# Last MoE1 block with its output product two tiles behind, layer 2's first weights loaded at once, y loads moved up

## The chip, the cores and the metric

One core of one Trainium2 chip runs the whole program in one launch. The metric is the device time of one execution in microseconds, as the median of several runs. The profile is one execution, taken by the hardware profiler. TensorE (PE) multiplies matrices; VectorE (DVE), ScalarE (ACT) and GpSimd (POOL) do the elementwise work; SyncE's queue (SP) issues nearly all DMAs. Each engine runs its own queue in order.

## The reference, cut to what matters

```python
attn_out = _attn_ref(q, k, v)                      # pooled + local attention, (4, 8, 576, 64)
x = attn_out.transpose(0, 2, 1, 3).reshape(2304, 512)
# MoE1: 512 -> 1536 -> 512
g = x @ w_gate
silu = g * (1.0 / (1.0 + np.exp(-g)))
y = silu * (x @ w_val) @ w_out
# MoE2 (layer 2): 512 -> 2048 -> 512
h = y @ w_in
g = np.maximum(h, 0.0) + alpha * np.minimum(h, 0.0)
out = g @ w_out2
```

Activations are float32 and the weights are float64, read on the chip as pairs of 32-bit words.

## The kernel before

**Products.** A float32 product is made of three TensorE products of operands split into a high and a low part: hi x hi, hi x lo, lo x hi (L488 to L490 in MoE1, L875 to L877 in layer 2). The high part is a cast on ACT, the low part a subtraction on POOL. Each float64 weight tile is first put together as float32: two ACT passes over the raw words (L656, L660), a merge on DVE (L664), then cast and subtraction (L687, L691). A loaded and split weight tile lives in a named SBUF place, `g0` to `g11`, `v0` to `v11`, `o0` to `o11`; a raw load (`w_load`) and its split result take places of that list.

**MoE1.** The tokens are 8 blocks of 288. For each block and each of 12 feature tiles j of 128: `m_g` (12 products, then `u`: tanh on ACT L531 and a DVE operation L532), `m_v` (12 products, then `u` on DVE L539, `ph` on ACT L542, `pl` on POOL L543), and `m_y`, the output product of the tile before (12 products into the PSUM tiles `Y`). So the order on TensorE is g(j), v(j), y(j-1). In the last block, g and v have four PSUM banks instead of two. The block's result is copied (L565) and written to `y1` in DRAM (L566).

**Layer 2, first product.** It runs as steps (token pair-block i of 576, weight pair q of 256 features), 32 of them, in the order of `VISITS`: i=0 with q 0 to 3, i=1 with q 0 to 7, i=0 with q 4 to 7, then i=2 and i=3. A step uses the seven-product scheme P1 to P7 of 2x2 blocks: six TensorE products each, with copies on ACT between them (L911 behind P1, L929 behind P6, L920 behind P7, L940 behind P5). `close` adds P4 and P3 of the step before, `prelu` applies the activation on DVE (L892, L893) and stores to `hbuf`. Its operands are sums and differences of weights (`conv_w`, L695 to L702) and of y (`prep_y`, L810, cast L796, low part L803 or L806). They are prepared in the background from the last MoE1 block on. For q above 4 the sums and differences of the weights run on POOL, else on DVE. The second product is `m2_out`, with weights from `conv_o`.

**The planner.** From the last MoE1 block on, the order on every queue is the order in which the program emits instructions. Background work is a list of tasks with engine, cost, inputs, earliest time `at` and due time. `tick` advances a planned clock (0.80 us for six products of 288 columns; it starts at 0 with the block) and `run_bg` goes through the tasks in order of due time: a task is emitted when its inputs are planned to end within LA and its engine is planned to be free within LB.

```python
COST = dict(A=lambda n: 0.2 + 0.00075 * n, D=lambda n: 0.14 + 0.0011 * n, P=lambda n: 0.05 + 0.0025 * n, S=lambda n: 5.0)
...
                if t["at"] > now or any(d["end"] is None or d["end"] > now + LA for d in t["deps"]):
                    continue
                if t["e"] != "S" and free.get(t["e"], 0.0) > now + LB:
```

`S` is a load: its cost is the planned time until the data have landed. A0 is the planned start of layer 2. `prod` forces whatever it needs that has not been emitted. Places: `PAIR` names, for each weight pair, the places of its raw loads and of its results, `X5S` those of its P7 operand, `YS` those of the first set of y operands.

Of the kernel before, what the change touches and what calls it, by code (L numbers as in the profile page):

```python
# [10 lines left out]
I32 = mybir.dt.int32  # L11
# [12 lines left out]
def attn_moe_moe2_kernel(  # L24
# [72 lines left out]
    wdma = {}  # L97
    W = {}

    def w_load(kind, j, slot):  # L100
        t = raw[slot] = wp.tile([128, 512, 2], I32, tag=slot, name="raw")
        src = wsrc[kind]
        if kind in ("o", "o2"):
            r = nc.sync.dma_start(out=t.rearrange("p f t -> p (f t)"), in_=src[j * 128:(j + 1) * 128, :])
        else:
            r = nc.sync.dma_start(
                out=t.rearrange("p f t -> p (f t)").rearrange("p (k f) -> p k f", k=KD),
                in_=src[:, j * 256:(j + 1) * 256].rearrange("(k p) f -> p k f", p=128))
        wdma[slot] = r.ins
# [424 lines left out]
    def m_v(blk, j):  # L534
        xh, xl = xt(blk)
        G = GB[2 * (j % 2) + 1] if blk == NB1 - 1 else GV[1]
        proj(G, HB, W[f"v{j}"][:, 0], W[f"v{j}"][:, 1], xh, xl)
        u = hid.pop((blk, j))
        nc.vector.scalar_tensor_tensor(out=u, in0=u, scalar=0.5, in1=G[:, :HB], op0=ALU.mult, op1=ALU.mult)  # L539
        ph = hp_.tile([128, HB], F32R, tag="ph", name="ph")  # L540
        pl = hp_.tile([128, HB], F32R, tag="pl", name="pl")
        nc.scalar.copy(out=ph, in_=u)  # L542
        nc.gpsimd.tensor_sub(pl, u, f32(ph))  # L543
        hid[blk, j] = (ph, pl)

    def m_y(blk, j):
# [7 lines left out]
        if j == F1 - 1:  # L554
# [16 lines left out]
    NQ = F2 // 2  # L571
    TB = 2 * HB
    NB2 = NT // TB
    PAIR = [("v0", "g1", "o0"), ("v1", "g2", "o1"), ("g3", "v3", "o2"), ("g4", "v4", "o3"),
            ("g8", "v8", "o7"), ("g9", "v9", "o8"), ("g10", "v10", "o9"), ("g11", "v11", "o10")]
    X5S = ["g0", "v2", "v7", "o11"]
    YS = ["g5", "v5", "o4", "o5", "g6", "v6", "g7", "o6"]
    VISITS = [(0, 0, 4), (1, 0, 8), (0, 4, 8), (2, 0, 8), (3, 0, 8)]
    YSET = (0, 1, 1, 0)
    GB = []  # L580
    SETS = []
    hbuf = dp.tile([F2 * 128, NT], F32, name="hbuf")

    A0 = 59.2
    LA, LB = 0.6, 0.8
    clock = [0.0]
    free = {}
    tasks = []
    due = [0.0]
    COST = dict(A=lambda n: 0.2 + 0.00075 * n, D=lambda n: 0.14 + 0.0011 * n, P=lambda n: 0.05 + 0.0025 * n, S=lambda n: 5.0)  # L590

    def bg(eng, n, fn, *deps, at=0.0):
        t = dict(e=eng, d=COST[eng](n), fn=fn, deps=deps, at=at, end=None, due=due[0])
        tasks.append(t)
        tasks.sort(key=lambda x: x["due"])
        return t

    def run_bg(flush=False):
        now = clock[0]
        busy = set()  # L600
        for t in list(tasks):
            if not flush:
                if t["e"] in busy:
                    continue
                if t["at"] > now or any(d["end"] is None or d["end"] > now + LA for d in t["deps"]):
                    continue
                if t["e"] != "S" and free.get(t["e"], 0.0) > now + LB:
                    busy.add(t["e"])
                    continue
            start = max([now, 0.0 if t["e"] == "S" else free.get(t["e"], 0.0)] + [d["end"] for d in t["deps"]])  # L610
            t["end"] = start + t["d"] + 0.15
            if t["e"] != "S":
                free[t["e"]] = start + t["d"]
            tasks.remove(t)
            t["fn"]()
# [15 lines left out]
    def tick(n, w):  # L631
        clock[0] += n * (0.0096 + 0.0004286 * w)
        run_bg()
# [10 lines left out]
    def unpack(kind, j, slot, which):  # L644
        z = {}

        def load():
            w_load(kind, j, slot)
            z["r"] = raw.pop(slot)

        def bits():
            n = 768 if which else 512
            z["t"] = side2.tile([128, n], F32, tag=f"st{which}", name="st", bufs=1)
            st = z["st"] = z["t"][:, 0:512]
            hw = z["r"][:, :, 1]
            nc.scalar.activation(out=st, in_=hw.bitcast(F32), func=AF.Prelu, scale=2.0 ** -112, alpha=-2.0 ** 32)  # L656

        def top():
            z["sk"] = side2.tile([128, 512], I32, tag="sk", name="sk", bufs=1)
            nc.scalar.activation(out=z["sk"], in_=top_byte(z["r"]), func=AF.Copy, scale=1.0 / 32, bias=-31.0 / 64)  # L660

        def merge():
            sti = z["st"].bitcast(I32)
            nc.vector.scalar_tensor_tensor(out=sti, in0=sti, scalar=3, in1=z["sk"],  # L664
                                           op0=ALU.logical_shift_left, op1=ALU.bitwise_or)

        return z, load, bits, top, merge

    def conv_w(q, at):
# [2 lines left out]
        s = PAIR[q]  # L672
        z0, load0, bits0, top0, merge0 = unpack("i2", 2 * q, s[0], 0)
        z1, load1_, bits1, top1, merge1 = unpack("i2", 2 * q + 1, s[1], 1)
        home = (s[2], s[1], s[0])
        x = {}
        val = {0: lambda: z0["st"], 1: lambda: z1["t"][:, 256:768], 2: lambda: z0["v"], 5: lambda: z1["t"][:, 0:256]}

# [44 lines left out]
        o1 = bg("P", 512, lo(1), h1)  # L723
        o2 = bg("P", 512, lo(2), h2)
        wt[q] = dict(P1=o0, P2=o0, P4=o1, P5=o1, P6=o2, P3=o2, P7=o5)
        held.update(st0=[h0, o0, df], st2=[h2, o2], st1=[h1, o1, h5, o5, df], sk=[m_])

    def conv_o(q, at):
        due[0] = A0 + 179.2 + 11.0 * q
        s = PAIR[q]  # L730
        ops = []
        for e, home in ((0, s[2]), (1, s[0])):
            z, load, bits, top, merge = unpack("o2", 2 * q + e, s[e], e)

            def hi(z=z, home=home):
                z["w"] = wp.tile([128, 2, 512], F32R, tag=home, name="w2")
# [38 lines left out]
    def prep_y(i, at, late, late0=None):  # L775
# [56 lines left out]
        o5 = bg("P", n, lo("P5", "11"), h5)  # L832
        yt[i] = dict(P1=o1, P2=o2, P3=o3, P7=o7, P6=o6, P4=o4, P5=o5)
        held["kn"] = [o7, o6, o4, o5]

    def again_p5(i, at, late):
        due[0] = late
# [70 lines left out]
    def step(s):  # L908
# [4 lines left out]
        tick(6, HB)  # L913
        if s:
            close(s - 1)

        def p7():
            prod(c, i, q, "P7", False)
            e = E7[s] = side2.tile([128, HB], F32, tag="e7", name="e7", bufs=2)
            nc.scalar.copy(out=e, in_=c)  # L920
            crit("A", 288, 0.8)
            tick(6, HB)

        if s == 0:
            p7()
            m_y(*fts[-1])
            open2()
        prod(t, i, q, "P6", True)
# [5 lines left out]
        tick(6, HB)  # L934
        prod(a, i, q, "P2", True)
        tick(6, HB)
        if s:
            p7()
        prod(b_, i, q, "P5", True)
        nc.scalar.copy(out=c, in_=b_)  # L940
        crit("A", 288, 0.8)
# [45 lines left out]
    if True:  # L987
# [141 lines left out]
        for i, (blk, j) in enumerate(fts):  # L1129
            if blk == NB1 - 1 and j == 0:  # L1130
# [5 lines left out]
                GB += [GV[0], GV[1], *[pa2.tile([128, 512], F32, name=f"h{e}") for e in range(2)]]  # L1136
                ctx.enter_context(tc.manual_schedule())
                live.append(1)
                for q in range(3):
                    conv_w(q, 0.8 * (10 + 9 * q))  # L1140
                prep_y(0, 0.8 * 26, 0.0, (29.6, 39.2))
                for q in range(3, 6):
                    conv_w(q, 0.8 * (37, 55, 61)[q - 3])
            if blk == 0:
                while pc[0] <= min(j + K["early"], F1 - 1):
                    prep1(pc[0])
# [17 lines left out]
            if last:  # L1164
# [1 line left out]
                crit("A", 288, 0.8)  # L1166
                crit("P", 288, 1.4)
                tick(6, HB)
            if i > 0:
                m_y(*fts[i - 1])  # L1170
            run(3 * i + 2)
            if last:
                tick(6, HB)
        gstack.close()
        pa3 = ctx.enter_context(tc.tile_pool(name="pa3", bufs=1, space=PSUM))
        SETS += [tuple(pa3.tile([128, 2, 512], F32, name=f"c{e}") for e in range(2)), (Y[0], Y[1])]
# [9 lines left out]
        for v, (i, q0, q1) in enumerate(VISITS):  # L1186
            now, end = clock[0], clock[0] + 5.58 * (q1 - q0)
            if v == 0:
                prep_y(1, now + 3.0, end + 1.6)
                for q in range(6, NQ):  # L1190
                    conv_w(q, now)
            elif v == 1:
                again_p5(0, end - 12.0, end)
                prep_y(2, end, end + 5.58 * 4)
            elif v == 3:
                prep_y(3, now, end)
# [49 lines left out]
```

## Time and profile before

| | us |
|---|---|
| median of 3 runs | 1003.16 |
| lowest and highest | 1002.13 and 1003.58 |
| the profiled execution | 1002.88 |
| its span, first to last instruction | 1001.1 |
| TensorE busy | 956.8 (96%) |
| VectorE, ScalarE, GpSimd busy | 494.6, 382.0, 458.5 |
| mean granted TensorE clock | 0.99 of full |

All times in the rows count from the start of the span. The last MoE1 block begins at 541.18. TensorE's products are pipelined: each row's length is longer than the distance of two starts, so the pace is read from the starts.

### The profile page before, as it was taken

To read this page: it belongs to the slowest core of one execution; us is meant where nothing else is said; L and a number is where in the kernel's file an instruction comes from. 1 tells how busy PE (TensorE), PEld (TensorE's weight loads), DVE (VectorE), ACT (ScalarE), POOL (GpSimd) and SP (SyncE) were. 2 spreads that over 40 slices of the span, in tenths; PEclk is the share of its full clock that TensorE was granted. 3 is DMA by queue.
4 is the path that set the end of the run, shared out by engine and by line. 5 is a ranking of instruction groups with operands and counts; after the bars stand their busy time and mean duration, and the time that the engine had idled before them with its cause. 6 is when DMAs were issued, how large, how long until landed. Compare 5 with 4: busy or idle time off the path is not lost.

```text
span 1001.1 us, 20369 instructions
## 1 busy us (share of the span) xinstructions
PE 956.8 (96%) x8144; PEld 883.8 (88%) x8144; DVE 494.6 (49%) x990; ACT 382.0 (38%) x876; POOL 458.5 (46%) x551
## 2 busy tenths in 40 slices
PE   5699899999999999999999988999999999999998
PEld 4589789999999999999999987999999887888886
DVE  5886874464535554444531564778566741010010
ACT  5698632222222222222222546544334574131231
POOL 6488853234322334222221586854511297444542
PEclk9989999999999999999999998999999999999999
DMA  7999731132111221111101644252425773353242
GB/s 192 266 335 332 176 89 34 27 80 58 37 42 33 69 47 41 45 23 20 43 9 41 200 126 137 96 190 95 143 107 204 246 241 123 89 184 99 91 131 100
DMA packets 151702, 116.22 MB, mean 116 GB/s; under 512 B 98873, under 2 KB 130617, under 8 KB 150841
## 3 DMA queue, kind: packets, MB, share of 16 engines
q1 hardware_dynamic: 151543, 114.92, 37.9%
q8 instruction: 63, 1.03, 0.4%
q14 instruction: 32, 0.26, 0.1%
q10 hardware_dynamic: 64, 0.01, 0.0%
HBM read 86.58 MB, written 34.60 MB: 121 GB/s over the span
## 4 chain that ended last, share of the span: by engine, by line
PE 76%; DVE 6%; DMA 6%; SPq 4%; POOL 3%; issue 3%; ACT 2%; DVEq 0%; POOLq 0%; ACTq 0%
PE y L488 7%; PE y L490 7%; PE y L489 7%; PE g L488 4%; PE v L489 4%; PE v L488 4%; PE g L489 4%; PE g L490 4%; PE v L490 4%; PE c L490 4%; PE c L489 4%; PE c L488 4%; PE c L875 3%; PE y L875 3%; PE c L876 3%
## 5 line engine op out<-in xcount | busy, mean ns | idle before, releaser
L961 POOL TENSOR_TENSOR hs<-hr,hs 128x512 fp32r<-128x512 f32 x72 | 96.6, 1358 | 84.8 <-ACT hs L960 84.8
L543 POOL TENSOR_TENSOR pl<-u,ph 128x288 fp32r<-128x288 f32 x96 | 81.5, 849 | 81.5 <-ACT ph L542 81.2
L489 PE MATMUL y<-pl,w 128*128 128x288 f32 x384 | 115.4, 302 | 2.5 <-POOL pl L543 2.5
L488 PE MATMUL g<-xh,w 128*128 128x288 f32 x360 | 109.9, 305 | 8.1 <-DVE u L532 3.8
L532 DVE SCALAR_TENSOR_TENSOR u<-u,g 128x288 f32<-128x288 f32 x90 | 40.7, 452 | 150.9 <-ACT u L531 150.7
L488 PE MATMUL y<-ph,w 128*128 128x288 f32 x384 | 113.1, 305 | 1.8 <-ACT ph L542 1.8
L490 PE MATMUL y<-ph,w 128*128 128x288 f32 x384 | 114.3, 300 | 0.0
L488 PE MATMUL v<-xh,w 128*128 128x288 f32 x360 | 108.9, 303 | 0.1
L489 PE MATMUL v<-xl,w 128*128 128x288 f32 x360 | 108.4, 301 | 0.0
L490 PE MATMUL g<-xh,w 128*128 128x288 f32 x360 | 107.3, 298 | 1.2 <-POOL qT L294 1.2
L489 PE MATMUL g<-xl,w 128*128 128x288 f32 x360 | 107.4, 298 | 0.0
L490 PE MATMUL v<-xh,w 128*128 128x288 f32 x360 | 106.8, 297 | 0.2 <-POOL w L143 0.2
L960 ACT CAST hs<-hr 128x512 fp32r<-128x512 f32 x72 | 41.7, 617 | 112.1 <-PE y L489 98.5
L531 ACT ACTIVATE u<-g 128x288 f32<-128x288 f32 x90 | 36.7, 408 | 122.4 <-PE g L490 118.9
L542 ACT CAST ph<-u 128x288 fp32r<-128x288 f32 x96 | 41.4, 432 | 104.8 <-DVE u L539 104.7
L981 DVE COPY os<-c 128x512 f32<-128x512 f32 x5 | 3.5, 691 | 156.7 <-PE c L490 156.7
L488 PEld LDWEIGHTS g<-xh,w 128*128 128x128 f32 x360 | 68.4, 190 | 11.3 <-DVE u L532 5.0
L488 PEld LDWEIGHTS y<-ph,w 128*128 128x128 f32 x384 | 71.8, 190 | 6.9 <-issue 4.4
L489 PEld LDWEIGHTS y<-pl,w 128*128 128x128 f32 x384 | 73.3, 191 | 3.9 <-POOL pl L543 3.6
L490 PEld LDWEIGHTS y<-ph,w 128*128 128x128 f32 x384 | 73.3, 191 | 0.9
L489 PEld LDWEIGHTS v<-xl,w 128*128 128x128 f32 x360 | 68.5, 190 | 1.6
L490 PEld LDWEIGHTS g<-xh,w 128*128 128x128 f32 x360 | 68.7, 191 | 1.4 <-POOL qT L294 1.4
(252 smaller groups left out, 2691.0 us busy)
## 6 DMA issues: line engine op xcount, KB each, us to landing
hbuf<-t SPq DMA_DIRECT2D x64, 288.0 KB
hr<-hbuf SPq DMA_DIRECT2D x36, 512.0 KB
raw<-in_moe_w_out_dram SPq DMA_DIRECT2D x28, 512.0 KB
raw<-in_moe_w_in_dram SPq DMA_DIRECT2D x16, 512.0 KB
raw<-in_moe_w_gate_dram SPq DMA_DIRECT2D x12, 512.0 KB
raw<-in_moe_w_val_dram SPq DMA_DIRECT2D x12, 512.0 KB
vw<-vwin SPq DMA_DIRECT2D x48, 96.0 KB
sy<-y SPq DMA_DIRECT2D x8, 576.0 KB
```

The costliest lines, as they stand in the source:

```text
L488: nc.tensor.matmul(o, lhi, rhi, start=first, stop=False)
L489: nc.tensor.matmul(o, lhi, rlo, start=False, stop=False)
L490: nc.tensor.matmul(o, llo, rhi, start=False, stop=last)
L531: nc.scalar.activation(out=u, in_=G[:, :HB], func=AF.Tanh, scale=0.5)
L532: nc.vector.scalar_tensor_tensor(out=u, in0=u, scalar=1.0, in1=G[:, :HB], op0=ALU.add, op1=ALU.mult)
L542: nc.scalar.copy(out=ph, in_=u)
L543: nc.gpsimd.tensor_sub(pl, u, f32(ph))
L875: nc.tensor.matmul(o, whi[:, ks], yhi[k], start=first, stop=False, skip_group_check=True)
L876: nc.tensor.matmul(o, whi[:, ks], ylo[k], start=False, stop=False, skip_group_check=True)
L960: nc.scalar.copy(out=h, in_=r)
L961: nc.gpsimd.tensor_sub(l, r, f32(h))
L981: nc.vector.tensor_copy(os_, bank[m])
```

## The change

In the last MoE1 block the output product of tile j is issued two tiles behind (after v(j+2)); tile 1 has none, and behind the loop stands that of tile 10, while that of tile 11 stands in layer 2's first step, directly behind P1. `ph` and `pl` of that block take a tile of the `t2` tag (three buffers). In the first step P7 moves from behind P1 to behind P2, where it stands in all others. Raw weights of pair 0 go into the tiles `sy0` and `sy1` (the y operands' landing place) and are asked for at 0.0. The places of all others are named anew, the times `at` are set anew, and the second y block's load is asked for inside the last MoE1 block, with its casts from 62.0 on. The planner's costs change: ACT, DVE (25% more for what is due early), loads 8.0 instead of 5.0; tasks due within 6 us may be emitted 0.8 us earlier, and DVE may be filled 1.4 us ahead once layer 2 has begun.

```diff
-    def w_load(kind, j, slot):
-        t = raw[slot] = wp.tile([128, 512, 2], I32, tag=slot, name="raw")
+    def w_load(kind, j, slot, pool=wp):
+        t = raw[slot] = pool.tile([128, 512, 2], I32, tag=slot, name="raw", bufs=1)
...
-        ph = hp_.tile([128, HB], F32R, tag="ph", name="ph")
-        pl = hp_.tile([128, HB], F32R, tag="pl", name="pl")
+        if blk == NB1 - 1:
+            t = side2.tile([128, 2, HB], F32R, tag="t2", name="pp", bufs=3)
+            ph, pl = t[:, 0], t[:, 1]
+        else:
+            ph = hp_.tile([128, HB], F32R, tag="ph", name="ph")
+            pl = hp_.tile([128, HB], F32R, tag="pl", name="pl")
...
-    PAIR = [("v0", "g1", "o0"), ("v1", "g2", "o1"), ("g3", "v3", "o2"), ("g4", "v4", "o3"),
-            ("g8", "v8", "o7"), ("g9", "v9", "o8"), ("g10", "v10", "o9"), ("g11", "v11", "o10")]
-    X5S = ["g0", "v2", "v7", "o11"]
-    YS = ["g5", "v5", "o4", "o5", "g6", "v6", "g7", "o6"]
+    PAIR = [("sy0", "sy1", "v0", "g1", "v1"), ("g2", "v2", "o0", "v2", "g2"), ("g3", "v3", "o1", "v3", "g3"), ("g4", "v4", "g5", "v4", "g4"),
+            ("g8", "v8", "o7", "v8", "g8"), ("g9", "v9", "o8", "v9", "g9"), ("g10", "v10", "o9", "v10", "g10"), ("g11", "v11", "o10", "v11", "g11")]
+    X5S = ["g0", "o2", "o6", "o11"]
+    YS = ["v5", "o3", "g6", "v6", "o4", "g7", "v7", "o5"]
...
-    A0 = 59.2
+    A0 = 57.5
     LA, LB = 0.6, 0.8
+    LBD = 1.4
...
-    COST = dict(A=lambda n: 0.2 + 0.00075 * n, D=lambda n: 0.14 + 0.0011 * n, P=lambda n: 0.05 + 0.0025 * n, S=lambda n: 5.0)
+    COST = dict(A=lambda n: 0.2 + 0.00082 * n, D=lambda n: 0.16 + 0.0011 * n, P=lambda n: 0.05 + 0.0025 * n, S=lambda n: 8.0)
...
-        t = dict(e=eng, d=COST[eng](n), fn=fn, deps=deps, at=at, end=None, due=due[0])
+        t = dict(e=eng, d=COST[eng](n) * (1.25 if eng == "D" and due[0] < A0 + 20.0 else 1.0), fn=fn, deps=deps, at=at, end=None, due=due[0])
...
-                if t["at"] > now or any(d["end"] is None or d["end"] > now + LA for d in t["deps"]):
+                more = 0.8 if t["due"] < now + 6.0 else 0.0
+                if t["at"] > now or any(d["end"] is None or d["end"] > now + LA + more for d in t["deps"]):
                     continue
-                if t["e"] != "S" and free.get(t["e"], 0.0) > now + LB:
+                if t["e"] != "S" and free.get(t["e"], 0.0) > now + (LBD if t["e"] == "D" and now > A0 else LB) + more:
...
+        if q == 0:
+            held["kn"] = [k0, k1]
...
-        if s == 0:
-            p7()
+        else:
             m_y(*fts[-1])
             open2()
         prod(t, i, q, "P6", True)
...
         prod(a, i, q, "P2", True)
         tick(6, HB)
-        if s:
-            p7()
+        prod(c, i, q, "P7", False)
+        e = E7[s] = side2.tile([128, HB], F32, tag="e7", name="e7", bufs=2)
+        nc.scalar.copy(out=e, in_=c)
+        crit("A", 288, 0.8)
+        tick(6, HB)
...
-                for q in range(3):
-                    conv_w(q, 0.8 * (10 + 9 * q))
-                prep_y(0, 0.8 * 26, 0.0, (29.6, 39.2))
-                for q in range(3, 6):
-                    conv_w(q, 0.8 * (37, 55, 61)[q - 3])
+                for q in range(NQ):
+                    conv_w(q, (0.0, 11.6, 16.4, 21.2, 40.4, 45.2, 50.0, 54.8)[q])
+                    if q == 3:
+                        prep_y(0, 20.0, 0.0, (31.0, 37.4))
+                        y1p5 = prep_y(1, 40.0, 1e6, (62.0, 62.0))
...
-            if i > 0:
-                m_y(*fts[i - 1])
+            if i > 0 and not (last and j == 1):
+                m_y(*fts[i - 2 if last and j else i - 1])
+                if last:
+                    tick(6, HB)
             run(3 * i + 2)
-            if last:
-                tick(6, HB)
+        m_y(*fts[-2])
+        tick(6, HB)
...
             if v == 0:
-                prep_y(1, now + 3.0, end + 1.6)
-                for q in range(6, NQ):
-                    conv_w(q, now)
+                y1p5["at"] = end + 1.6
             elif v == 1:
-                again_p5(0, end - 12.0, end)
+                again_p5(0, end - 20.0, end)
```

`conv_w` and `conv_o` take their places from the longer `PAIR` entries; `prep_y` returns the task that casts P5, so that its time can be set later.

## Rows read from the trace of the kernel before

**Rows 1.** Windows: length, busy us (instructions) of each engine, granted clock, DMA.

```profile
574.80:599.20 24.40, 21.52 (x145) 20.62 (x144) 15.63 (x21) 13.18 (x27) 19.48 (x19) 0.93 0.39 114
599.20:616.00 16.80, 12.46 (x69) 11.63 (x68) 8.49 (x15) 8.80 (x21) 12.01 (x12) 0.80 0.32 103
616.00:640.00 24.00, 24.00 (x180) 23.78 (x180) 16.03 (x22) 14.28 (x32) 20.56 (x16) 1.00 0.40 140
...
704.00:720.00 16.00, 14.20 (x96) 13.96 (x95) 8.93 (x12) 4.86 (x11) 8.14 (x9) 0.89 0.45 149
```

**Rows 2.** TensorE's timeline: start us, length us, instruction [idle before it].

```profile
541.18 0.29 PE L488 MATMUL g<-xh,w 128*128 128x288 f32 x1
...
545.98 0.30 PE L488 MATMUL h<-xh,w 128*128 128x288 f32 x1
...
602.36 0.29 PE L490 MATMUL h<-xh,w 128*128 128x288 f32 x1
...
610.49 0.44 PE L876 MATMUL c<-yq,x 128*128 128x288 f32 x1
...
615.53 0.44 PE L876 MATMUL c<-yq,w 128*128 128x288 f32 x1
...
616.00 0.30 PE L875 MATMUL c<-yq,w 128*128 128x288 f32 x1
```

**Rows 3.** TensorE's waits, 520 to 720 us: total, times, longest.

```profile
PE c L875 <- DVE u L539: 2.5, 1, 2.5
...
PE y L488 <- ACT ph L542: 1.8, 2, 1.6
PE y L489 <- POOL pl L543: 1.7, 3, 0.6
PE c L875 <- ACT c L911: 1.3, 1, 1.3
```

**Rows 4.** Timelines of GpSimd (first row) and VectorE.

```profile
592.22 3.06 POOL L691 TENSOR_TENSOR w<-st,w 128x512 fp32r<-128x512 f32 x2
...
592.29 3.61 DVE L810 TENSOR_TENSOR sy<-sy 128x576 f32<-128x576 f32 x2 [1.12 <-POOL yq L803]
...
607.18 0.44 DVE L539 SCALAR_TENSOR_TENSOR u<-u,h 128x288 f32<-128x288 f32 x1
...
612.27 0.43 DVE L702 TENSOR_TENSOR st<-st 128x256 f32<-128x256 f32 x1
```

**Rows 5.** The page's costliest groups: busy us, mean ns.

```profile
L543 POOL TENSOR_TENSOR pl<-u,ph 128x288 fp32r<-128x288 f32 x96 | 81.5, 849 | 81.5 <-ACT ph L542 81.2
...
L542 ACT CAST ph<-u 128x288 fp32r<-128x288 f32 x96 | 41.4, 432 | 104.8 <-DVE u L539 104.7
```

**Rows 6.** Timelines of SyncE, ScalarE and TensorE around 710 us.

```profile
706.57 0.93 SPq L784 DMA_DIRECT2D sy<-y  x2
...
713.17 0.67 ACT L796 CAST yq<-sy 128x576 fp32r<-128x576 f32 x1 [1.23 <-DMA sy<-y]
713.75 0.39 ACT L929 COPY y<-y 128x288 f32<-128x288 f32 x1
...
714.20 0.40 PE L875 MATMUL y<-yq,w 128*128 128x288 f32 x1 [1.80 <-ACT y L929]
```

**Rows 7.** Timelines of ScalarE and TensorE around 779 us.

```profile
778.52 0.67 ACT L656 ACTIVATE st<-raw 128x512 f32<-128x512 f32 x1 [2.18 <-DMA raw<-in_moe_w_out_dram]
...
779.94 0.40 PE L875 MATMUL c<-yq,w 128*128 128x288 f32 x1 [0.83 <-ACT c L940]
```

**Rows 8.** VectorE's groups, 541.2 to 616 us, shapes kept apart.

```profile
L664 DVE SCALAR_TENSOR_TENSOR st<-st,sk 128x512 int32<-128x512 int32 x10 | 9.3, 930 | 6.9 <-ACT sk L660 6.7
...
L695 DVE TENSOR_TENSOR st<-st 128x256 f32<-128x256 f32 x5 | 5.0, 1006 | 0.1
```

**Rows 9.** GpSimd's groups, 610 to 640 us.

```profile
L691 POOL TENSOR_TENSOR w<-st,w 128x512 fp32r<-128x512 f32 x4 | 5.7, 1424 | 5.1 <-PE c L877 3.0 <-ACT w L687 2.0
L695 POOL TENSOR_TENSOR st<-st 128x256 f32<-128x256 f32 x1 | 0.7, 743 | 0.0
```

More of the change, by code (lines that the diff above doesn't have):

```diff
@@ L647, in load @@
         def load():
-            w_load(kind, j, slot)
+            w_load(kind, j, slot, side2 if slot[0] == "s" else wp)
             z["r"] = raw.pop(slot)
@@ L674, in conv_w @@
         z1, load1_, bits1, top1, merge1 = unpack("i2", 2 * q + 1, s[1], 1)
-        home = (s[2], s[1], s[0])
+        home = s[2:]
         x = {}
@@ L731, in conv_o @@
         ops = []
-        for e, home in ((0, s[2]), (1, s[0])):
-            z, load, bits, top, merge = unpack("o2", 2 * q + e, s[e], e)
+        for e, home in ((0, s[2]), (1, s[3])):
+            z, load, bits, top, merge = unpack("o2", 2 * q + e, s[3 + e], e)
             def hi(z=z, home=home):
@@ L834, in prep_y @@
         held["kn"] = [o7, o6, o4, o5]
+        return h5
     def again_p5(i, at, late):
@@ L915, in step @@
             close(s - 1)
[L917 to L921, printed above, removed]
-            tick(6, HB)
-        if s == 0:
-            p7()
+        else:
             m_y(*fts[-1])
@@ L1168, in attn_moe_moe2_kernel @@
                 tick(6, HB)
-            if i > 0:
-                m_y(*fts[i - 1])
+            if i > 0 and not (last and j == 1):
+                m_y(*fts[i - 2 if last and j else i - 1])
+                if last:
+                    tick(6, HB)
             run(3 * i + 2)
-            if last:
-                tick(6, HB)
+        m_y(*fts[-2])
+        tick(6, HB)
         gstack.close()
```

## The prediction

> **What bounds the kernel now.** I read the table of stages first, then TensorE's waits, then its timeline, and last the queues that it waits for. From 616 to 640 us TensorE is busy 24.00 of 24.00 us at full clock; in the two stages before it has 21.52 of 24.40 and 12.46 of 16.80, at mean granted clocks of 0.93 and 0.80, and from 704 to 720 it has 14.20 of 16.00 at 0.89 [rows 1]. So the loss near the change lies in the last MoE1 block and in one place of layer 2; elsewhere only a faster TensorE would help.
>
> The size of the first loss follows from counting. The first product of the block starts at 541.18; 36 products later, at 545.98, the next tile begins: 4.80 us a tile, 0.133 us a product [rows 2]. From 541.18 to the end of P6 of layer 2's first step (616.00) stand 12 x 36 + P1, P7 and P6 of 6 each + the last output product of 12 = 462 products, 61.6 us. The trace has 74.8. **13.2 us are lost.** The waits name 2.5 + 1.8 + 1.7 + 1.3 = 7.3 us of it [rows 3]: output products that wait for `ph` (ACT, L542) and `pl` (POOL, L543), layer 2's P1 that waits for the last `u` (DVE, L539), and its copy. Most of the rest is half speed after two of the stalls: 21 starts between 610.49 and 615.53 are 0.24 us apart [rows 2].
>
> Why are `ph` and `pl` late? TensorE ends the last `v` at about 602.6 (its last product starts at 602.36 [rows 2]), but its `u` runs at 607.18 on DVE, 4.6 us later [rows 4]. DVE runs in order, and conversion work stands ahead: two differences of the y preparation took 3.61 us there from 592.29 on, while POOL worked on its own (592.22, 3.06 us) [rows 4].
>
> **The change part by part.** *Output product two tiles behind.* Behind `v` of tile j stand in the old order the output product of j-1, then `g` and `v` of j+1, so 4.8 us until its own output product. `u`, `ph` and `pl` take 0.44 + 0.43 + 0.85 = 1.7 us [rows 4, 5]. A lag of DVE above 3.1 us therefore stalls TensorE, and 4.6 is there. In the new order 9.6 us lie between, and the lag may be 7.9. The number of products is the same; behind the last `v` stand the output products of tiles 9 and 10 (24 products, 3.2 us), then P1. `ph` and `pl` move to three buffers, as many as are in flight: tile j takes the place of j-3, whose product was issued a tile earlier. That new wait costs nothing unless TensorE itself is a tile late.
>
> *Weights 0 at once.* Their raw data go to `sy0` and `sy1`, free since attention ended, instead of places that tiles 0 and 1 still use. The planner had them asked at 8.0 us of the block and counted 5.0 for landing, and now asks at 0 and counts 8.0: their conversion starts some 5 us earlier. Weights 1 to 3 and the first y follow at 11.6 to 21.2 us, so all that layer 2's first four steps need is planned before about 50. The two SP issues of weights 0 pass the two y1 writes of the block before; neither waits for the other's data.
>
> *Second y load.* Its two SP issues stand at 40 us instead of behind the last block's four y1 writes. They wait for the first y's subtractions on POOL, and the raw loads of weights 4 to 7 stand behind them, which layer 2 wants only from step 4. The second y's casts are planned from 62 us on, against about 65 before (asked at 57.5 + 3.0, 5.0 for the load). Taken as 0, since step 4, its first user, starts near 80 in both plans; if that cover is gone, step 4 waits.
>
> *Step 0's P7 behind P2.* The last output product now follows P1 directly, with 0.8 us less cover; step 1's P1, which reuses the Y banks, has 0.8 more. Sum 0, but the lag that the last tile may have is small: `v` of 11, two output products (3.2), P1 (0.8) make 4.0, less 1.7 is 2.3 us for the output product; P1 itself, behind 3.2 us and one `u`, bears 2.7.
>
> *Planner's costs.* A load now counts as 8.0 us instead of 5.0, so what uses it is put 3.0 us later. That reaches two stalls outside the block. Last y load (token block 3): issued at 706.57, landed only for the cast at 713.17; the cast stands ahead of ACT's copy L929, P5 waits for that 1.80 us [rows 6], and 16 us at 0.89 of the clock lose another 1.8 [rows 1]. Three us are three or four slots of 0.80 us, which puts the casts behind L929 of that step: **3.6 us** come back. Output weights: ACT waits 2.18 us for raw data, and P2 or P5 of the step 0.83 [rows 7]: **0.8 us**. Here nothing but ACT's queue is passed.
>
> *What it adds.* Weights 4 to 7 are crowded closer to the end of the block and into steps 0 to 4, and VectorE may be filled 1.4 us ahead instead of 0.8. How late DVE then is at tile 11 no row shows. Below: 0, since the work needed early is done by 50 us and the queue can empty before weights 4 arrive at 48.5. Above: all that the end of the block costs today, 2.5 + 1.3 of waits [rows 3] and 22 products at 0.107 us extra, 6.1 us. Nearest row: weights 4's six DVE operations. In this block a merge took 0.93 on average and the first sum 1.01 [rows 8], while the shortest difference took 0.43 [rows 4]. The planner counts 0.82 for two sums or differences and 0.72 for a merge, so two pairs at 2.0 and two merges make DVE up to 2 x 1.2 + 2 x 0.2 = 2.8 us late, 0.5 more than the 2.3 allowed. I add 0.5 for ACT, where urgent casts may now stand 1.4 us ahead of their input. **Residual 1.0 us.**
>
> The Trainium skill speaks against this part: GPSIMD Engine Reference, Key points, says that GpSimd shares its SBUF interfaces with VectorE and contends with DVE instructions that have two SBUF inputs. The trace agrees: two differences took 3.61 us beside a POOL subtraction [rows 4]. By that rule all four sums and differences of weights 4 slow down, and the residual is the 1.0 above; without it DVE is in time and the residual is ACT's 0.5.
>
> **Sum.** 13.2 + 3.6 + 0.8 = 17.6 gained, 1.0 given back. The profiled execution took 1002.88 (span 1001.1), 0.3 under the median of the runs: 1002.9 - 16.6 = **986.3 us**.
>
> **The rivals.** *The three engines pace the block, not the order of the products.* If the lag at tile 11 stays near 4.6, P1 and the last output product stall as now: at most the 6.1 us above, 985.3 + 6.1 = 991.4; at half of it, without the clock, 988. For it: weights 4 and 5 run there in both plans. Against: the lag of today was brought by y differences at 592, which now come before 45 us of the plan (586). Chance 0.24.
>
> *Steps 0 to 5 stall.* POOL is already busy 20.56 of 24.00 us from 616 to 640 [rows 1] and gets weights 5 to 7 in the same stretch; ACT's copy for P5 has 1.6 us of cover. Two stalls of the size of 1.8 with their half speed, 3.6 each, give at most 7: 988 to 993. Against: today's same density costs TensorE nothing there. Chance 0.12.
>
> *The longer load count does nothing for the last y.* If its load is put later by as much as its cast, 3.6 stay: 989.9. Chance 0.06.
>
> *Slower.* `pl` of tile 11 stands behind weights 5 to 7 on POOL. Each has three large subtractions of 1.42 and five small operations of 0.74, 8.0 us there [rows 9], 23.9 for three; less the 2.3 allowed the last output product waits 21.6, and the kernel takes about 986.3 + 21.6 = 1008. It decides once more than 17.6 + 2.3, about 20 us of POOL work are ahead. Against: weights 6 and 7 are asked at 50.0 and 54.8 and counted as landed 8 us later, behind the last `v` at 54.3. Chance 0.04. That all this changes nothing (another wait takes the whole place): 0.02.
>
> **How the numbers follow.** 0.52 for the forecast, 985.3 to 988. From 0.2% (2.0 us, about what a measurement can tell from no change here): faster 0.94, same 0.02, slower 0.04. The range begins at 984.0 (985.3 with no residual, and the lowest run lies 0.75 below the profiled one) and ends at 992.5, which takes in the first three rivals but for a tail of the second; about 0.1 is left out.
>
> **What would show it.** In the block: no wait for L542 or L543 before the last tile; 36 products in 4.80 us throughout; the first step's P6 ending near 541 + 62; the last y's casts behind L929 and no gap near 695; full clock from 540 to 760. Wrong if `g` products wait for `u` (the pace theory), if P1 or the last output product stalls over 2 us, or if step 4 waits for a y cast.

## The result and the profile after

The changed kernel takes **992.98 us** (median of 4 runs, 992.42 to 994.23), the kernel before 1003.37 beside it: ratio 0.990, 95% interval 0.9883 to 0.9917. That is 10 us faster, where 16.6 were forecast, and 0.5 us outside the range. The profiled execution took 992.76, with a span of 991.0.

The stages of the kernel after, beside [rows 1] (length, busy us of TensorE, its weight loads, VectorE, ScalarE, GpSimd, granted clock, DMA):

```profile
574.80:599.20 24.40, 24.40 (x185) 24.40 (x184) 15.71 (x22) 13.16 (x27) 22.13 (x21) 1.00 0.53 160
599.20:610.40 11.20, 8.96 (x53) 7.94 (x51) 6.62 (x11) 8.22 (x20) 7.70 (x8) 0.85 0.59 187
610.40:640.00 29.60, 29.60 (x223) 29.60 (x224) 22.59 (x29) 19.61 (x42) 25.59 (x21) 1.00 0.27 101
...
704.00:720.00 16.00, 16.00 (x122) 15.99 (x121) 10.66 (x15) 8.18 (x18) 13.69 (x13) 1.00 0.33 124
```

TensorE now runs through the block at full clock until 599, and through 704 to 720. What is left of the first loss lies between 599.2 and 610.4. TensorE's waits of the kernel after, first 520 to 720 us (beside [rows 3]), then from 720 to the end:

```profile
PE c L884 <- DVE u L539: 1.4, 1, 1.4
PE c L884 <- ACT c L920: 0.4, 1, 0.4
PE c L884 <- ACT c L943: 0.2, 1, 0.2
PE y L489 <- POOL pp L547: 0.2, 1, 0.2
...
PE c L490 <- POOL hs L964: 3.0, 4, 1.1
```

The output products' waits for `ph` and `pl` are gone but for 0.2 us. P1 of layer 2's first step still waits for the last `u`, 1.4 us instead of 2.5. The last row lies in the second product of layer 2 (`hs` is the low part of its hidden values). In the kernel before, from 720 us to the end, that wait was small:

```profile
PE c L490 <- POOL hs L961: 0.4, 1, 0.4
```

To see where the 10 us come from I cut each trace at four places of TensorE's timeline: the start of the last MoE1 block, the first product of layer 2's second step, the last product of the first-product stage, and the end. From the block's start to the second step stand 474 products, 63.2 us at 0.1333 each; what the stretch takes beyond that is called the **block's loss** below.

| us | before | after | difference |
|---|---|---|---|
| start of the block | 541.18 | 541.91 | +0.7 |
| block's loss | 13.46 | 4.04 | -9.4 |
| steps (second step to last product) | 180.41 | 176.20 | -4.2 |
| from there to the end | 202.85 | 205.65 | +2.8 |
| span | 1001.1 | 991.0 | -10.1 |

The segments are those of one execution each, the profiled one. The start of the block lies between 540.6 and 544.3 in the kernels below, with no edit ahead of it, so I compare the other three segments besides the times.

**What is left of the block's loss.** TensorE's timeline of the kernel after around layer 2's first step, beside [rows 2]:

```profile
599.38 0.30 PE L490 MATMUL y<-pp,w 128*128 128x288 f32 x1
601.05 0.37 PE L884 MATMUL c<-yq,w 128*128 128x288 f32 x1 [1.38 <-DVE u L539]
...
603.06 0.45 PE L490 MATMUL y<-pp,w 128*128 128x288 f32 x1
...
604.50 0.45 PE L490 MATMUL y<-pp,w 128*128 128x288 f32 x1
605.37 0.61 PE L884 MATMUL c<-yq,w 128*128 128x288 f32 x1 [0.43 <-ACT c L920]
```

1.67 us pass between the first two starts, where 0.13 would do. The seven starts from 603.06 to 604.50 are 0.24 apart: half speed. Then P6 waits for the copy of P1. The timelines of GpSimd (first two rows), ScalarE (next three) and VectorE in the kernel after tell why P1 waits:

```profile
594.79 1.29 POOL L697 TENSOR_TENSOR w<-st,w 128x512 fp32r<-128x512 f32 x1
...
596.80 2.99 POOL L697 TENSOR_TENSOR w<-st,w 128x512 fp32r<-128x512 f32 x2
...
596.11 0.67 ACT L662 ACTIVATE st<-raw 128x512 f32<-128x512 f32 x1 [1.71 <-POOL w L697]
596.68 0.65 ACT L666 ACTIVATE sk<-raw 128x512 int32<-128x512 uint8 x1
597.23 0.40 ACT L531 ACTIVATE u<-h 128x288 f32<-128x288 f32 x1
...
597.44 1.21 DVE L670 SCALAR_TENSOR_TENSOR st<-st,sk 128x512 int32<-128x512 int32 x1 [3.51 <-ACT sk L666]
598.57 0.44 DVE L532 SCALAR_TENSOR_TENSOR u<-u,h 128x288 f32<-128x288 f32 x1
598.93 1.15 DVE L701 TENSOR_TENSOR st<-st 128x256 f32<-128x256 f32 x1
600.12 0.42 DVE L702 TENSOR_TENSOR st<-st 128x256 f32<-128x256 f32 x1
600.46 0.45 DVE L539 SCALAR_TENSOR_TENSOR u<-u,h 128x288 f32<-128x288 f32 x1
```

VectorE is idle for 3.51 us, and then does the whole of a tile's work at once. It waited for ScalarE's pass L666 of weights 3, which stood behind L662, which waited until GpSimd's L697 (594.79) had freed its place. In the meantime the last tile's tanh (L531) stood behind both passes. So a late subtraction on GpSimd reaches TensorE through two other queues: GpSimd, ScalarE, VectorE, P1. The last `u` starts 4.2 us behind the end of its product, against 4.7 before.

**The second product.** GpSimd's timeline of the kernel after, and below it TensorE's:

```profile
806.90 1.29 POOL L964 TENSOR_TENSOR hs<-hr,hs 128x512 fp32r<-128x512 f32 x1 [1.86 <-issue]
808.15 3.00 POOL L748 TENSOR_TENSOR w<-st,w 128x512 fp32r<-128x512 f32 x2
811.11 2.68 POOL L964 TENSOR_TENSOR hs<-hr,hs 128x512 fp32r<-128x512 f32 x2
...
812.44 0.50 PE L490 MATMUL c<-w,hs 128*128 128x512 f32 x1 [1.08 <-POOL hs L964]
```

The same stretch of the kernel before:

```profile
810.69 1.74 POOL L961 TENSOR_TENSOR hs<-hr,hs 128x512 fp32r<-128x512 f32 x1
812.40 1.29 POOL L740 TENSOR_TENSOR w<-st,w 128x512 fp32r<-128x512 f32 x1
813.70 1.70 POOL L961 TENSOR_TENSOR hs<-hr,hs 128x512 fp32r<-128x512 f32 x1
815.35 1.29 POOL L740 TENSOR_TENSOR w<-st,w 128x512 fp32r<-128x512 f32 x1
```

Before, one subtraction of weights (`w`) alternates with one of hidden values (`hs`). After, two `w` stand ahead of two `hs`, and the product waits for the first of these, 1.08 us here. It waits for an `hs` at four places, 3.0 us in all, at three of them (812.44, 821.44, 828.89) for one that stands behind two `w`.

### The profile page after: what moved, and what is told of

Same layout as the page of the kernel before. It is cut to its first block, busy times and chain, and to the rows that moved or that the text cites. A ratio compares the mean times of both kernels' runs of the same rounds, so it can differ in the third digit from the quotient of the medians.

```text
span 991.0 us, 20390 instructions
## 1 busy us (share of the span) xinstructions
PE 951.9 (96%) x8144; PEld 881.6 (89%) x8144; DVE 493.1 (50%) x990; ACT 382.2 (39%) x876; POOL 457.5 (46%) x551
## 5 line engine op out<-in xcount | busy, mean ns | idle before, releaser
L964 POOL TENSOR_TENSOR hs<-hr,hs 128x512 fp32r<-128x512 f32 x72 | 93.7, 1318 | 88.5 <-ACT hs L963 86.4
L532 DVE SCALAR_TENSOR_TENSOR u<-u,g 128x288 f32<-128x288 f32 x90 | 40.7, 453 | 148.2 <-ACT u L531 148.1
L489 PE MATMUL y<-pl,w 128*128 128x288 f32 x336 | 99.5, 298 | 0.4 <-POOL pl L547 0.4
L490 PE MATMUL y<-ph,w 128*128 128x288 f32 x336 | 98.9, 297 | 0.0
L547 POOL TENSOR_TENSOR pl<-u,ph 128x288 fp32r<-128x288 f32 x84 | 70.4, 838 | 59.0 <-ACT ph L546 58.6
L488 PE MATMUL y<-ph,w 128*128 128x288 f32 x336 | 97.5, 302 | 0.0
L531 ACT ACTIVATE u<-g 128x288 f32<-128x288 f32 x90 | 36.9, 410 | 121.0 <-PE g L490 117.5
L546 ACT CAST ph<-u 128x288 fp32r<-128x288 f32 x84 | 36.3, 432 | 90.0 <-DVE u L539 90.0
L490 PEld LDWEIGHTS v<-xh,w 128*128 128x128 f32 x360 | 69.5, 193 | 1.2 <-POOL w L143 1.2
L488 PEld LDWEIGHTS v<-xh,w 128*128 128x128 f32 x360 | 69.3, 193 | 0.9 <-DVE u L539 0.3
L489 PEld LDWEIGHTS g<-xl,w 128*128 128x128 f32 x360 | 69.1, 192 | 0.0
```

The source lines that it names most:

```text
L488: nc.tensor.matmul(o, lhi, rhi, start=first, stop=False)
L489: nc.tensor.matmul(o, lhi, rlo, start=False, stop=False)
L490: nc.tensor.matmul(o, llo, rhi, start=False, stop=last)
L531: nc.scalar.activation(out=u, in_=G[:, :HB], func=AF.Tanh, scale=0.5)
L532: nc.vector.scalar_tensor_tensor(out=u, in0=u, scalar=1.0, in1=G[:, :HB], op0=ALU.add, op1=ALU.mult)
L964: nc.gpsimd.tensor_sub(l, r, f32(h))
```

## The experiments

Two theories stood at first. *Order*: the block's gain comes from the output product two tiles behind. *Pace* (the prediction's first rival): the lag of the three engines' queues sets it, and whatever shortens the queues brings the gain. "Lag" is the start of a tile's `u` (VectorE, L539) less the end of its second product, taken as the start of its last TensorE product plus 0.13 us. Tiles count from 0 to 11.

**1. The order alone**, on the kernel before (with the third buffer, and the casts of the first y at their new distance):

```diff
-            if i > 0:
-                m_y(*fts[i - 1])
+            if i > 0 and not (last and j == 1):
+                m_y(*fts[i - 2 if last and j else i - 1])
...
+        m_y(*fts[-2])
```

> The kernel before, with one part of the change: output products two tiles behind and three buffers for ph and pl; the first y casts are asked 4.8 us later (34.4 and 44.0), since their places o4 and o5 come free a tile later. Theory 'order' (the stalls come from the output product asking too early): the waits for ph and pl inside the block go, and only the end of the block still stalls (P1 for the last u, then half speed, 6 us): the loss between the block's first product and step 1 falls from 13.5 to 6 to 7 us, the time to 996 to 997. Rival 'pace' (ACT, DVE and POOL set the pace of the block): the loss stays above 11 us and the waits move to g products or to P1; 1001 to 1003.

1001.65 us, ratio 0.9998 (0.9987 to 1.0009): no change. The block's loss is 11.86 instead of 13.46. TensorE's waits of this kernel, 520 to 720 us:

```profile
PE c L879 <- ACT c L915: 2.4, 1, 2.4
PE y L489 <- POOL pp L547: 1.7, 1, 1.7
PE y L879 <- ACT y L933: 1.3, 1, 1.3
PE y L488 <- ACT pp L546: 1.3, 1, 1.3
PE c L879 <- DVE u L539: 0.8, 1, 0.8
```

With more room TensorE simply runs ahead until the queues are 8.4 us behind at the last tile (4.7 before), and then waits. On this kernel it is pace, not order.

**2. The kernel after with the output product one tile behind again:**

```diff
-            if i > 0 and not (last and j == 1):
-                m_y(*fts[i - 2 if last and j else i - 1])
+            if i > 0:
+                m_y(*fts[i - 1])
...
-        m_y(*fts[-2])
-        tick(6, HB)
```

> The changed kernel with its output products one tile behind again; all else stays. Theory 'order': DVE is 4 us late from tile 7 on here too, so output products wait for ph and pl again, 4 to 9 us more with the half speed, 997 to 1002. Rival 'schedule' (the earlier weights and the new times would have removed the stalls alone): within 1 us of the changed kernel, 992 to 994.

996.85 us, ratio 0.9946 (0.9931 to 0.996), 3.9 over the kernel after: between what the two theories expected. The block's loss is 4.07, as after, so inside the block the order is worth nothing here. The 3.9 come behind it: the steps take 180.54, with a wait of 2.55 us at 617.67 for the activation. VectorE's timeline of this kernel:

```profile
609.17 1.38 DVE L701 TENSOR_TENSOR st<-st 128x256 f32<-128x256 f32 x1
610.59 1.55 DVE L702 TENSOR_TENSOR st<-st 128x256 f32<-128x256 f32 x1
612.06 1.65 DVE L707 TENSOR_TENSOR st<-st 128x256 f32<-128x256 f32 x1
613.75 1.54 DVE L708 TENSOR_TENSOR st<-st 128x256 f32<-128x256 f32 x1
...
616.86 0.76 DVE L902 SCALAR_TENSOR_TENSOR t<-c,t 128x576 f32<-128x576 f32 x1
```

Four small operations fell into one stretch at 1.38 to 1.65 us each, where the shortest of them take 0.41. GpSimd ran without a pause beside them (608.93 to 616.56). In the kernel after it paused from 607.87 to 609.13, and the last three of the same four took 0.42 to 0.43 there; VectorE's timeline of the kernel after:

```profile
608.18 0.42 DVE L702 TENSOR_TENSOR st<-st 128x256 f32<-128x256 f32 x1
```

**3. Weights 4 to 7 asked later**, in the kernel after:

```diff
-                    conv_w(q, (0.0, 11.6, 16.4, 21.2, 40.4, 45.2, 50.0, 54.8)[q])
+                    conv_w(q, (0.0, 11.6, 16.4, 21.2, 52.0, 57.0, 62.0, 67.0)[q])
```

> The changed kernel with weights 4 to 7 asked at 52, 57, 62 and 67 instead of 40.4 to 54.8. Theory 'weights 4 and 5 stand ahead of the last u': P1's wait (1.4) and the one behind it go, no half speed there, the loss from the block's first product to step 1 falls from 4.0 to below 1.5; 989.5 to 990.5. Rival 'tail of the first y' (POOL and DVE are late from its preparation): P1 still waits over 1 us; 993. Second rival: the same work stalls steps 1 to 8 instead, 993 or more, with waits of TensorE between 610 and 650.

995.36 us, ratio 0.993 (0.9913 to 0.9946). P1's wait stays at 1.37 us and the last lag at 4.1, so weights 4 do not make it, against my prediction. The rest of the block's end clears (loss 2.06), but 2.3 us of wait for the activation and 0.7 for a copy appear at 622 and 619: steps 180.51. So the time is not the 989.5 to 990.5 of the theory but that of the second rival (993 or more).

**4. Load count 5.0 for the output weights**, all else as after:

```diff
         ls = [bg("S", 0, o[0], at=at) for o in ops]
+        for t in ls:
+            t["d"] = 5.0
```

> The changed kernel with the planner's load count of 5.0 for the output weights alone (8.0 for all others). Theory 'load count': ScalarE's and GpSimd's order in the second product is again one output weight, one split of h in turn, TensorE's four waits for hs (3.0 us) go, and the wait near 766 for raw output weights (1.0) comes back: 2 us less, about 991. Rival (the waits for hs come from the earlier start of the second product against its loads): the waits stay, 993 to 994.

989.82 us, ratio 0.9873 (0.9856 to 0.9889). The `hs` waits are gone, the end takes 202.60 instead of 205.65. A wait of 0.44 us near 767 for the copy behind P5 is back, and the steps take 177.15 instead of 176.20. So the longer count has two effects on the output weights, and the larger is a loss.

**5. Nothing in the background on ACT and DVE from 48.9 to 54.2 of the planned clock:**

```diff
-                if t["e"] in busy:
+                if t["e"] in busy or (t["e"] in "AD" and 48.9 < now < 54.2):
```

The shifted plan makes one P3 product of layer 2 read the y operand of the next token block, so what it computes is not the reference. That product stands in the steps, at 126 us of the planned clock, far behind the block.

> The changed kernel, in which the planner emits no background work on ScalarE and VectorE between planned 48.9 and 54.2, so that nothing of it stands between the v of tile 10 and the last u. Theory 'weights 3 ahead of the last u' (a merge and two sums of weights 3 stand there now): the last u runs less than 1 us behind its v instead of 4.2, P1 and the last output product do not wait, no half speed; the loss from the block's first product to step 1 falls from 4.0 to below 1, and the time to 989.5 to 990.5. Rival 'put off': weights 3, put off by 5 us, come late for step 3 or crowd VectorE in steps 1 to 3; TensorE waits over 2 us between 610 and 630, 992 to 995.

1000.06 us, ratio 0.9974 (0.9962 to 0.9987). The last lag falls to 0.2 us and the block's loss to 0.69, the lowest of all: weights 3 ahead of the last `u` are the cause of what was left. But the last casts of weights 4 to 7 come 7 to 10 us later in the plan, and new waits in the steps (7.2 us in all up to 720, the longest 2.1) cost more than that: steps 184.92. The time is above what either theory expected.

**6. The old costs of ACT and DVE in the kernel after** (no 25%, no lead of 0.8, VectorE filled 0.8 ahead; load count 8.0 kept):

```diff
-    COST = dict(A=lambda n: 0.2 + 0.00082 * n, D=lambda n: 0.16 + 0.0011 * n, ...
+    COST = dict(A=lambda n: 0.2 + 0.00075 * n, D=lambda n: 0.14 + 0.0011 * n, ...
...
-                more = 0.8 if t["due"] < now + 6.0 else 0.0
+                more = 0.0
```

> The changed kernel with the planner's old costs for ScalarE and VectorE, no 25% and no earlier or deeper filling (load count stays 8.0). Theory 'times': the early start and the new places and times removed the lag; the lag of u stays at or below 5 us, the loss to step 1 at or below 5, 992 to 995. Rival 'costs': it was the planner's higher costs that thinned the queues; the lag grows above 6 us at tiles 9 to 11 and the loss to step 1 above 7, 996 to 1000.

1000.01 us, ratio 0.9974 (0.9964 to 0.9985). The block's loss is 10.32, the last lag 8.8; steps (175.71) and end (206.76) are nearly those of after. VectorE's timeline of this kernel:

```profile
589.36 3.61 DVE L818 TENSOR_TENSOR sy<-sy 128x576 f32<-128x576 f32 x2 [1.40 <-POOL yq L811]
592.89 0.44 DVE L539 SCALAR_TENSOR_TENSOR u<-u,h 128x288 f32<-128x288 f32 x1
...
602.93 0.46 DVE L532 SCALAR_TENSOR_TENSOR u<-u,h 128x288 f32<-128x288 f32 x1 [3.01 <-ACT u L531]
603.49 0.81 DVE L670 SCALAR_TENSOR_TENSOR st<-st,sk 128x512 int32<-128x512 int32 x1
604.21 0.44 DVE L539 SCALAR_TENSOR_TENSOR u<-u,h 128x288 f32<-128x288 f32 x1
```

The y differences stand ahead of a `u` at 589 again, as in [rows 4]. VectorE is idle for 3 us as well: it is not short of time, its queue and ScalarE's are in a bad order.

**7. The load count 8.0 alone**, on the kernel before:

```diff
-    COST = dict(..., S=lambda n: 5.0)
+    COST = dict(..., S=lambda n: 8.0)
```

> The kernel before with the planner's load count 8.0 instead of 5.0 and nothing else. Theory 'load count': the wait for the last y near 712 goes (3.6 us with its half speed) and the one near 778 (1.0), the second product gets four waits for hs (2.9 us more); from step 1 on 1.7 us less. In the block the weights are converted 3 us later, so its loss stays 12 to 15: 1000 to 1003. Rival: the load count also thins the block's queues, and its loss falls below 10; below 999.

1003.03 us, ratio 1.0006 (0.9994 to 1.0017). The last-y stall and the one near 778 are gone (steps 177.59, 2.8 less, with a new wait of 1.0 us), the block loses 3.1 less (10.41, where the theory had 12 to 15 and the rival less than 10), and the end takes 206.71, 3.9 more. The block started 3.1 us later in the profiled execution, which takes back what its segments gained.

**8. Weights 0 asked at 8.0 instead of 0.0** in the kernel after:

```diff
-                    conv_w(q, (0.0, 11.6, 16.4, 21.2, ...
+                    conv_w(q, (8.0, 11.6, 16.4, 21.2, ...
```

> The changed kernel with weights 0 asked at 8.0 instead of 0.0. Theory 'head start': weights 0 then run into weights 1 and 2, the lag of u at tiles 6 to 11 grows by 2 us or more and the loss to step 1 from 4.0 to 6 or 7; 995 to 997. Rival (weights 0 have room either way, the limit is POOL between 20 and 50): the lag and the loss stay within 1 us; 992 to 994.

998.43 us, ratio 0.9958 (0.9946 to 0.9971), 5.45 over the kernel after and above what either theory expected. The block loses 5.46, 1.4 more than after; the lags of tiles 9 and 10 grow from 3.7 and 2.0 us to 4.4 and 5.2, that of tile 11 falls from 4.2 to 2.2. The steps take 180.44, with a wait of 2.2 us for the activation. The early load is worth having, but it is not the 9.4 us.

**9 to 12.** Two questions were left: whether the costs do it alone, and whether the rest of the losses can be had back.

*9. Load count 8.0 for the first two pairs of output weights, 5.0 for the other six*, in the kernel after:

```diff
+        for t in ls:
+            t["d"] = 8.0 if q < 2 else 5.0
```

> The kernel after, with the load count of the output weights at 8.0 for the first two pairs and 5.0 for the other six. Theory: the long count does two separate things; it keeps the first pair's passes out of ACT's way (the wait near 766 us) and it breaks the alternation of weight and hidden-value work on GpSimd (the waits for the subtraction L964). Then both are gone: from layer 2's last first-product to the end 202.6 us as with 5.0 throughout, steps 176.2 as in the kernel after, median near 989 us. Rival: two pairs with the long count are enough to break the alternation: 205 to 206 us for the second product, 992 to 993 in all.

989.77 us, ratio 0.9869 (0.9852 to 0.9885). Steps 176.45, end 202.43: both waits are gone, as the theory has it. In time it is level with experiment 4.

*10. The new ACT and DVE costs alone*, on the kernel before:

```diff
-    COST = dict(A=lambda n: 0.2 + 0.00075 * n, D=lambda n: 0.14 + 0.0011 * n, ...
+    COST = dict(A=lambda n: 0.2 + 0.00082 * n, D=lambda n: 0.16 + 0.0011 * n, ...
...
-        t = dict(e=eng, d=COST[eng](n), ...
+        t = dict(e=eng, d=COST[eng](n) * (1.25 if eng == "D" and due[0] < A0 + 20.0 else 1.0), ...
```

> The kernel before with nothing but the planner's new ACT and DVE costs (25% more for what is due early, the 0.8 us of lead for tasks due within 6 us, DVE filled 1.4 us ahead in layer 2); load count, order, places and times as before. Theory (the length of the ACT and DVE queues sets the end of the block): the loss in the block falls from 13.5 to 7 or 8 us, the last u of the block is less than 4 us behind its product, and about 997 us come out, with the wait for the last y still there. Rival (the costs thin the queues only together with the new times of the loads): the loss stays at 12 to 13.5 us, 1001 to 1003 in all.

999.32 us (11 runs), ratio 0.9965 (0.9952 to 0.9977). The block's loss falls from 13.46 to 8.87: 4.6 us for changed numbers in a plan, with the products in their old order. That is less than the 6 expected, and the last lag (4.8) did not shrink; the lags of tiles 7 and 8 did, from 5.6 and 5.9 to 2.0 and 2.7. The traces show why. Ahead of the `u` of tile 7 VectorE had done 20 background operations of this block and ScalarE 26 in the kernel before; here it is 15 and 22. Ahead of the last `u` it is 29 and 41 before and 28 and 40 here, nearly the same, and so is the lag.

*11. The same with the output product two tiles behind:*

> The kernel before with the new ACT and DVE costs of the last kernel and the output product two tiles behind. Theory (the order is worth little at any length of the queues): within 1 us of the kernel with the costs alone, in the block and in all. Rival (the order pays once the queues are shorter than the 9.6 us that it gives): the block loses 3 us less than with the costs alone or better, 994 or less if that one is at 997.

996.42 us (6 runs), ratio 0.9935 (0.9921 to 0.995). The block's loss is 7.31, 1.6 less than in experiment 10: the same 1.6 as between the kernel before and experiment 1. In time the two kernels are 2.9 apart; the profiled spans are 2.8 apart, of which 1.0 is the start of the block. So neither expectation holds: not under 1 us, and not 3.

*12. Experiment 9 with a shorter hold of ACT and DVE:*

```diff
-                if t["e"] in busy:
+                if t["e"] in busy or (t["e"] in "AD" and 50.0 < now < 52.8):
```

> The kernel with the mixed load count (8.0 for two pairs of output weights), and ACT and DVE background work held back for 2.8 us of the planned clock (50.0 to 52.8) instead of 5.3. Theory: weights 3 ahead of the last u cost about 3 us in the block; a hold of half the length takes most of that away (loss 1 to 2.5 us instead of 4.0) and delays weights 7 by 6 us in the plan, which is still ahead of its step, so the steps stay at 176 to 178: 986 to 988. Rival: any delay of weights 4 to 7 comes back as waits in the steps, as the long hold showed (184.9 there): steps of 180 or more, 990 or above.

989.36 us, ratio 0.9864 (0.9849 to 0.988): the lowest, but level with experiment 9 and above the 986 to 988 expected. VectorE's timeline of this kernel:

```profile
596.50 0.46 DVE L532 SCALAR_TENSOR_TENSOR u<-u,h 128x288 f32<-128x288 f32 x1 [3.24 <-ACT u L531]
597.05 0.46 DVE L539 SCALAR_TENSOR_TENSOR u<-u,h 128x288 f32<-128x288 f32 x1
597.42 1.79 DVE L670 SCALAR_TENSOR_TENSOR st<-st,sk 128x512 int32<-128x512 int32 x1
```

The last `u` now stands ahead of the merge of weights 3, not behind it. P1's wait is gone and the block's loss is 1.55. The steps give 1.4 back (177.83, a wait of 1.3 us for the activation).

## Why the prediction was right and wrong

**Right: where the losses are.** The 13.2 us of the block, the last-y stall and the output weights' wait were real and could be recovered. Experiment 5 reached 0.69 us of loss in the block, though no kernel here had all of it back at once.

**The step that failed: "Output product two tiles behind".** I gave this edit the whole 13.2 us, by comparing the room it makes (4.8 to 9.6 us) with a lag of 4.6 taken as fixed. The lag is not fixed. TensorE's stalls held it at 4.6; without them TensorE runs ahead and the lag grows to 8.4 (experiment 1). The order alone takes 1.6 us off the block and nothing off the time. Where the queues are thinner it is worth something in time, 2.9 us in experiment 11 against 10 and 3.9 in the kernel after against experiment 2, there by a wait behind the block. The first rival, that the engines pace the block, is what happened.

What brought the 9.4 us, as the experiments add it up: the planner's costs 4.6 (10 against before), the order 1.6 (11 against 10), and by difference 3.3 for the new load times, places and load count together, which were not run as a group (the load count alone took 3.1 off the block of the kernel before, experiment 7). Counted from the other end the costs are worth 6.3 (6 against after), the early weights 0 1.4 (8), the order 0 (2). The parts thus overlap.

How the costs act can be counted in the traces: by the rule in `run_bg` higher costs let fewer background operations be emitted ahead of a `u`. With the old costs VectorE and ScalarE did 29 and 41 ahead of the last `u` (experiment 6), in the kernel after 26 and 36, and the last lag is 8.8 and 4.2 us.

That the forecast of the block came near (12.2 us, measured 9.4) is luck: the gain was given to the order, and parts to which the prediction gave nothing in the block brought most of it. None of the prediction's signs of being wrong showed in the kernel after (P1 waited 1.4 us, the last output product 0.2, no `g` product at all); it took experiments 1 and 10 to tell the two theories apart.

My argument against that rival was that today's lag came from the y differences at 592, and that these now come before 586 us. The trace before spoke against the first half already: the longest lag, 5.9 us, is that of tile 8, whose `u` (first row, kernel before) ran ahead of them. In the kernel after they run at 586.63 (second row), and in the last five tiles the lags are 2.0 to 4.2: they moved, and weights 3 came into their place.

```profile
588.59 0.44 DVE L539 SCALAR_TENSOR_TENSOR u<-u,v 128x288 f32<-128x288 f32 x1
...
586.63 3.27 DVE L818 TENSOR_TENSOR sy<-sy 128x576 f32<-128x576 f32 x2 [1.74 <-POOL yq L811]
```

**"Residual 1.0 us" was 4.0, and from another source.** I looked for it in weights 4's operations on VectorE. Experiment 3 moved weights 4 away and P1's wait stayed; experiments 5 and 12 moved weights 3 and it went. I had all that the first four steps need "planned before about 50"; the plan in fact puts the last three casts of weights 3 at 54 to 56, and GpSimd is busy 22.13 of 24.40 us from 574.8 to 599.2, over half of it with the first y's subtractions. That makes L697 late, and behind it L662 and L666, one after another.

The Trainium skill's rule on shared interfaces (GPSIMD Engine Reference, Key points) holds in the rows above: the merge L670 and the sum L701 took 1.21 and 1.15 us while GpSimd ran until 599.8, the next sum 0.42 after it. I was right to hold it against this change; in the kernel after the operations that it hits ahead of the last `u` are those of weights 3, not of weights 4.

**"Planner's costs": right, and one side not counted.** The two waits came back as said: 3.6 + 0.8 = 4.4 forecast, 4.2 measured in the steps. SyncE issues the last y's load at 698.38, and ScalarE's casts run without a wait for it, behind a copy instead of ahead. ScalarE's timeline of the kernel after, beside [rows 6]:

```profile
705.11 0.38 ACT L943 COPY y<-y 128x288 f32<-128x288 f32 x1 [0.45 <-PE y L886]
705.40 0.68 ACT L804 CAST yq<-sy 128x576 fp32r<-128x576 f32 x1
705.98 0.40 ACT L920 COPY c<-c 128x288 f32<-128x288 f32 x1
```

But I wrote that "nothing but ACT's queue is passed". The count also moves the subtractions of the output weights on GpSimd, and these share a queue with the hidden values' (L964), for which TensorE waits. That cost 2.8 us; experiments 4, 7 and 9 show it from both sides.

**The sum.** Of the 6.5 us between 986.3 and the profiled 992.76, the block is 2.8 (9.4 instead of 12.2), the second product 2.8, the steps 0.2, and the start of the block 0.7, ahead of which no edit stands.

Two steps held as costed: the second y's load in its new place stalled nothing, and weights 5 to 7 did not put `pl` behind them on GpSimd, so the slower rival did not come.

**What stays open.** Which of the costs (ACT's, VectorE's, the 25%) does most was not tried apart. Nor was it tried to put the activation ahead of background work, though a wait for it (1.3 to 2.6 us) appears in experiments 2, 3, 8 and 12, in all of which the plan has work of weights 4 to 7 later than in the kernel after.

## What to carry to other kernels

A lag that is measured while the consumer stalls is held down by those stalls: before a deeper pipeline is credited with the whole stall, ask how fast the producers' queues run when nobody waits, and what stands ahead of the wanted operation on each of them. When a planner's constant changes, follow it on every queue that its tasks use, since here 3 us of load count gained 2.8 us in the steps (experiment 7), on ScalarE's queue, and lost 2.8 to 3.9 in the second product, on GpSimd's. Background work that is pushed out of one stall goes somewhere: every edit here that cleared the block's end further (2.06, 0.69, 1.55) gave time back in the steps.

## What the runs showed of the hardware

The stall at P1 is equally long in the kernel after and in experiment 9 (1.38 and 1.35 us), and the instructions up to there are the same. Yet from 599.2 to 610.4 us the granted clock was 0.85 in the one and 1.00 in the other. Experiment 9's stage and TensorE's timeline:

```profile
599.20:610.40 11.20, 8.26 (x55) 7.41 (x56) 5.78 (x11) 9.05 (x22) 7.96 (x8) 1.00 0.50 164
...
600.21 0.37 PE L886 MATMUL c<-yq,w 128*128 128x288 f32 x1 [1.35 <-DVE u L539]
...
604.51 0.40 PE L886 MATMUL c<-yq,w 128*128 128x288 f32 x1 [1.21 <-ACT c L922]
```

The block hardly differs (4.04 and 3.72 us of loss): without the half speed TensorE waits 1.21 us for the copy of P1 instead of 0.43, and P6 starts 4.3 us behind P1 in both. Half speed behind a stall is thus not pure loss where the next product waits anyway, and adding it to the waits when a stall is priced, as the prediction did for its bounds, can count one delay twice.

VectorE's operations with one input in PSUM were not stretched beside GpSimd: L532 took 0.44 us at 598.57, between a merge of 1.21 and a sum of 1.15.
